# Query features of the last three batches taken token-major and turned by the DMA crossbar, in a kernel of linear attention and a squared-ReLU layer

## The chip, the cores and the metric

The kernel runs on one core of a Trainium2 chip. The metric is the time of one execution on the device, in microseconds (us). The kernel before took 355.43 us, the median of three runs (355.03 to 355.8).

## The reference

The program is attention with learned exponential features, and behind it a two-layer network without bias. Inputs are q, k and v of 8 batches, 8 heads, 576 positions and 64 values per head, a feature matrix `w_phi` of 64 x 128, and the network's weights of 512 x 2048 and 2048 x 512.

```python
def phi(x):
    proj = np.einsum('bhsd,df->bhsf', x, w_phi)
    proj = proj - np.max(np.abs(proj), axis=-1, keepdims=True)
    return np.concatenate([np.exp(proj), np.exp(-proj)], axis=-1)
q_p, k_p = (phi(q), phi(k))
kv = np.einsum('bhsf,bhsd->bhfd', k_p, v)
z = np.sum(k_p, axis=2)
num = np.einsum('bhsf,bhfd->bhsd', q_p, kv)
den = np.einsum('bhsf,bhf->bhs', q_p, z)[..., None] + 1e-06
attn = num / den                       # 8 x 8 x 576 x 64
x = attn.transpose(0, 2, 1, 3).reshape(4608, 512)
out = np.maximum(x @ w_in, 0.0) ** 2 @ w_out
```

So a token's query is projected on 128 features, and the exponentials of the projection and of its negative are the two halves of its features. The shift by the largest absolute value needs that maximum for each token and head.

## The kernel before, in words

A batch has 576 positions: 512 in four groups and 64 left over. The attention of a batch works in chunks c = 0 to 4. Chunks 0 to 3 hold 128 tokens by 8 heads, as 4 columns of 128 by 2 halves (a pair of heads lies on the upper and the lower 64 partitions); chunk 4 holds the 64 tokens that are left, two heads stacked on the partitions.

For batches 2 to 7, k and q are loaded by POOL's DMA queue (L253, L261, L273) into `xk` and `xq`, two buffers each (batch b uses buffer b % 2), and turned to `kT` and `qT` by one DMA transpose for each tensor, issued by SP (`transposed`, L338). Then:

- **Keys** (`kgroup_ops`): TensorE projects a group token-major (`project`, L354: 8 matmuls of 64 rows, two heads at a time on the two halves of the array), VectorE takes the maximum (L409), ScalarE writes the two exponentials `kp` and `kn` (L415). `em_ops` and `v_ops` scale v by the exponential of the maximum into `va`; `kv_ops` (L472, L477) sums over the tokens, into `kv`.
- **Query maxima** (`qmax_ops`): the same projection token-major (L354, called Pq here), VectorE's maximum (L514, Mq), and ScalarE's exponential of minus twice the maximum (`en`, L521, L527). The projection is then thrown away.
- **Query features** (`q_ops`): TensorE projects the same queries a second time, now with the features on the partitions (L549, called Fq: two matmuls of 64 rows by 512 columns, 256 in chunk 4), and ScalarE writes the exponentials `qp` and `qn` (L564), 3 slots of each, used in turn.
- **Output** (`out_ops`): `qp` times `kv` on TensorE (L579, NA: 8 matmuls), VectorE multiplies the sum by `en` (L591, SA), `qn` times `kv` is added (L579, NB), VectorE divides (L599, L603) into `xo`, and SP turns `xo` by a DMA transpose (L637, Xx) into `xT`, or for chunk 4 into `xS`.

Batches 0 and 1 are turned on TensorE (L328) instead.

The network (`ffn_in`, L719, F1: four matmuls of 128 x 512 for one piece; `ffn_out`, L784, F2: four more) runs over chunks of 512 tokens. Chunk c of 0 to 7 is made of batch c's first 512 positions and needs all four pieces of `xT` before its first F1; chunk 8 is made of the 64 positions left in each batch (`xS`). `relu_sq` (L694, L696, L703) is between F1 and F2. Results leave through `ot` (L195, L197; 3 buffers) and a store that SP issues (L803).

Each operation is first recorded by `add` as a step with a number, in the order of the program. Then the lists at the end of the file decide: `ORDER` is the one sequence in which all 1731 steps are emitted, so it fixes each engine's own order (engines run in order and meet only on semaphores); `BASES` is the PSUM bank of each accumulation; `STATES` picks VectorE, ScalarE or GpSimd where a step may go to either; `GATES` ties single POOL loads to an earlier step. Attention of batch b + 1 is spread between the F1 and F2 steps of chunks b and b - 1.

Of the kernel before, what the change touches and what calls it, by code (L numbers as in the profile page):

```python
# [7 lines left out]
F32 = mybir.dt.float32  # L8
# [3 lines left out]
ACT = mybir.ActivationFunctionType  # L12
# [12 lines left out]
def dve_cost(n):  # L25
    return n / 960 + 0.064, n / 960 + 0.150 + SEM
# [85 lines left out]
def kernel(  # L112
# [41 lines left out]
    def sb(name, shape, dt=BF16):  # L154
        return pool.tile([P, *shape], dt, name=name)

    def ring(name, n, shape, dt=BF16):
        return [sb(f"{name}{i}", shape, dt) for i in range(n)]
# [19 lines left out]
    qp, qn = ring("qp", NQP, [8 * P]), ring("qn", NQP, [8 * P])  # L178
# [4 lines left out]
    mkn = sb("mkn", [36], F32)  # L183
# [132 lines left out]
    def attention(b):  # L316
# [181 lines left out]

        def qmax_ops(c):
# [17 lines left out]
            add("DVE", dve_cost(2 * n * Fd), fn, r=[pj], w=[("mq", s2, c)], closes=pj, what="Mq")  # L517
# [13 lines left out]

        qfeat = {}
# [128 lines left out]
        else:  # L661
# [17 lines left out]
            kv_ops(3)  # L679
            for c in range(5):  # L680
                qmax_ops(c)
            for c in range(5):
                q_ops(c)
                out_ops(c)
# [320 lines left out]
```

## Time and profile before

| | before |
|---|---|
| time, median of 3 runs | 355.43 us |
| span of the profiled execution (first to last instruction) | 353.0 us |
| median run less that span | 2.4 us |
| instructions | 8396 |
| TensorE matmul, weight load | 340.7 us, 192.2 us busy |
| VectorE, ScalarE, GpSimd | 276.1 us, 226.8 us, 96.6 us busy |
| DMA queue filled by software (POOL's loads) | 18.36 MB |
| DMA queue filled by hardware (SP: transposes and stores) | 20.42 MB |

In the profile PE is TensorE's matmul, PEld its weight load, DVE VectorE, ACT ScalarE, POOL GpSimd, and SPq the queue of DMA issues of SyncE. L549 is line 549 of the kernel. A row of a timeline gives start, length, engine, line, operation, tiles written and read, and count; in brackets stands the idle time of the engine before it and what ended that. Neighbouring instructions of one kind are merged in a row. Ends of matmuls are modelled, so the distance between two starts says more than a duration.

### The profile page before, as it was taken

How to read it: one execution, taken by the hardware profiler on the slowest of the kernel's cores; microseconds unless marked ns; L12 is line 12 of the kernel's file. 1: busy time of each engine (PE TensorE's matmuls, PEld its weight loads, DVE VectorE, ACT ScalarE, POOL GpSimd, SP SyncE). 2: the span in 40 equal slices, each digit the busy share in tenths (PEclk: the TensorE clock that was granted, in tenths of full speed). 3: DMA queues.
4: the chain of work that ended last, by engine and by line, in shares of the span. 5: the costliest groups of instructions: out<-in, count | busy, mean ns of one | idle time of the engine just before them, and what ended most of it. 6: DMA issues, size and time to landing. Idle time of an engine off the chain costs nothing.

```text
span 353.0 us, 8396 instructions
## 1 busy us (share of the span) xinstructions
PE 340.7 (97%) x3367; PEld 192.2 (54%) x3400; DVE 276.1 (78%) x524; ACT 226.8 (64%) x428; POOL 96.6 (27%) x144
## 2 busy tenths in 40 slices
PE   8889999999999999999999999999999999999995
PEld 5679875544654554545445654455555544444452
DVE  4999998899979988989678888799988727736210
ACT  4999887499688875785678577869676211340301
POOL 8745350488429300297001820000000000000000
PEclk9999999999999999999999999999999999999999
DMA  9999999899989976899354995600211211010105
GB/s 102 177 200 202 196 107 155 134 142 175 182 169 150 155 141 155 160 111 158 79 129 84 120 187 111 146 20 21 53 40 53 47 51 48 30 59 2 59 3 176
DMA packets 96101, 39.59 MB, mean 112 GB/s; under 512 B 64576, under 2 KB 91584, under 8 KB 96064
## 3 DMA queue, kind: packets, MB, share of 16 engines
q0 software_dynamic: 45216, 18.36, 45.6%
q1 hardware_dynamic: 50528, 20.42, 26.5%
q8 instruction: 26, 0.43, 0.5%
q10 hardware_dynamic: 320, 0.30, 0.3%
q14 instruction: 11, 0.09, 0.1%
HBM read 36.77 MB, written 9.44 MB: 131 GB/s over the span
## 4 chain that ended last, share of the span: by engine, by line
PE 79%; DVE 8%; ACT 6%; DMA 3%; issue 2%; SPq 0%; POOL 0%; DVEq 0%; ACTq 0%; POOLq 0%
PE psum L784 30%; PE psum L719 28%; PE psum L579 5%; PE psum L354 4%; PE psum L472 3%; PE psum L730 3%; PE psum L549 2%; DVE va L442 2%; DMA xq<-in_q_dram 1%; DVE mq L514 1%; ACT kp L415 1%; ACT kn L415 1%; DMA out_dram<-ot 1%; DVE mk L388 1%; DVE h L703 1%
## 5 line engine op out<-in xcount | busy, mean ns | idle before, releaser
L784 PE MATMUL psum<-wout,h 128*128 128x512 bf16 x527 | 128.4, 379 | 3.2 <-issue 1.3
L719 PE MATMUL psum<-xT,win 128*128 128x512 bf16 x448 | 106.1, 379 | 0.1
L694 ACT ACTIVATE hr<-psum 128x512 bf16<-128x512 f32 x96 | 55.3, 596 | 46.3 <-PE psum L719 24.3
L784 PEld LDWEIGHTS <-h 128*128 128x128 bf16 x560 | 50.2, 98 | 55.2 <-issue 2.0
L719 PEld LDWEIGHTS <-win 128*128 128x128 bf16 x512 | 47.4, 97 | 53.7 <-issue 3.1
L703 DVE TENSOR_TENSOR h<-hr 128x512 bf16<-128x512 bf16 x143 | 55.9, 415 | 16.4 <-ACT hr L694 15.6
L564 ACT ACTIVATE qp<-psum 128x1024 bf16<-128x1024 f32 (+1 forms) x40 | 37.4, 940 | 21.9 <-PE psum L549 21.5
L514 DVE TENSOR_REDUCE mq<-psum 128x8 f32<-128x1024 f32 (+1 forms) x40 | 44.1, 1110 | 4.0 <-PE psum L354 3.2
L409 DVE TENSOR_REDUCE mk<-psum 128x8 f32<-128x1024 f32 (+1 forms) x35 | 38.1, 1110 | 3.1 <-PE psum L354 3.1
L415 ACT ACTIVATE kp<-psum 128x1024 bf16<-128x1024 f32 (+1 forms) x35 | 32.8, 937 | 11.6 <-DVE mk L409 8.9
L564 ACT ACTIVATE qn<-psum 128x1024 bf16<-128x1024 f32 (+1 forms) x40 | 37.4, 939 | 1.3 <-PE psum L579 1.0
L696 DVE TENSOR_SCALAR hr<-psum 128x512 bf16<-128x512 f32 x48 | 32.6, 686 | 6.5 <-PE psum L719 5.2
L253 POOL DMA_DIRECT2D xv<-in_v_dram x26 | 19.4, 763 | 51.3 <-DVE va L442 48.0
L415 ACT ACTIVATE kn<-psum 128x1024 bf16<-128x1024 f32 (+1 forms) x35 | 32.8, 936 | 0.0
L442 DVE TENSOR_TENSOR va<-xv,va 64x256 bf16<-64x256 bf16 (+2 forms) x68 | 30.4, 462 | 1.6 <-ACT va L434 0.8
L591 DVE TENSOR_TENSOR psum<-psum,en 128x520 f32<-128x520 f32 (+1 forms) x40 | 27.6, 699 | 3.9 <-PE psum L579 2.5
L603 DVE TENSOR_TENSOR xo<-psum,rden 128x512 bf16<-128x512 f32 (+1 forms) x40 | 27.3, 686 | 1.0 <-DVE rden L599 0.2
L197 ACT ACTIVATE ot<-psum 128x512 f32<-128x512 f32 x18 | 10.7, 595 | 27.1 <-PE psum L784 27.1
L195 DVE COPY ot<-psum 128x512 f32<-128x512 f32 x17 | 11.5, 684 | 15.2 <-PE psum L784 7.9
L253 POOL DMA_DIRECT2D xk<-in_k_dram x28 | 20.6, 743 | 8.4 <-ACT va L428 4.0
L472 PE MATMUL psum<-va,kp 128*128 128x65 bf16 x256 | 19.6, 193 | 0.8 <-DVE va L442 0.4
L472 PE MATMUL psum<-va,kn 128*128 128x65 bf16 x256 | 19.6, 193 | 0.0
(69 smaller groups left out, 403.4 us busy)
## 6 DMA issues: line engine op xcount, KB each, us to landing
out_dram<-ot SPq DMA_DIRECT2D x32, 256.0 KB, 2.7
xk<-in_k_dram POOLq DMA_DIRECT2D x26, 128.0 KB, 4.3
xq<-in_q_dram POOLq DMA_DIRECT2D x24, 128.0 KB, 5.5
xv<-in_v_dram POOLq DMA_DIRECT2D x24, 128.0 KB, 4.2
win<-in_moe_w_in_dram POOLq DMA_DIRECT2D x4, 512.0 KB, 11.3
wout<-in_moe_w_out_dram POOLq DMA_DIRECT2D x4, 512.0 KB, 11.7
xq<-in_q_dram POOLq DMA_DIRECT2D x4, 256.0 KB, 5.8
xv<-in_v_dram POOLq DMA_DIRECT2D x2, 512.0 KB, 9.3
```

What stands on the lines that cost most here:

```text
L253: pin(nc.gpsimd.dma_start(out=x[:, a * 512 : z * 512].rearrange("p (h x) -> p h x", x=4 * D), in_=src[b][2 * a : 2 * z, 0:512, :].rearrang ...
L409: pin(nc.vector.tensor_reduce(out=mk_view(g), in_=ps2(pj)[:, :, : n * Fd].rearrange("p e (i f) -> p e i f", f=Fd), axis=AX.X, op=ALU.max, ...
L415: pin(nc.scalar.activation(out=dst[slot][:, :, :n, :].rearrange("p e i f -> p e (i f)"), in_=ps2(pj)[:, :, : n * Fd], func=ACT.Exp, scale= ...
L442: pin(engine().tensor_tensor(out=t[:, :, :D].rearrange("p m (x c) -> p m x c", c=2), in0=x.rearrange("p (m x c) -> p m x c", m=n, c=2), in ...
L472: pin(nc.tensor.matmul(out=o[:, sg, hi, :], lhsT=(kp, kn)[sg][kgroup[pr]][:, j % 2, 2 * hi + j // 2, :], rhs=va[s2][sg][:, 8 * pr + 4 * hi ...
L514: pin(nc.vector.tensor_reduce(out=mqb[:, c, :, :n], in_=ps2(pj)[:, :, : n * Fd].rearrange("p e (i f) -> p e i f", f=Fd), axis=AX.X, op=ALU ...
L564: pin(nc.scalar.activation(out=o, in_=i_, func=ACT.Exp, scale=sgn))
L694: pin(nc.scalar.activation(out=hr[sl], in_=ps1(g), func=ACT.Relu))
L696: pin(nc.vector.tensor_scalar(out=hr[sl], in0=ps1(g), scalar1=0.0, scalar2=None, op0=ALU.max))
L703: pin(engine().tensor_tensor(out=dst, in0=i_, in1=i_, op=ALU.mult))
L719: pin(nc.tensor.matmul(out=o, lhsT=win[mc // 4][:, kc, mc % 4 * P : (mc % 4 + 1) * P], rhs=x, start=(kc == 0), stop=(kc == KC - 1)))
L784: pin(nc.tensor.matmul(out=ps1(g), lhsT=h2[c % 2][mc // 4][:, mc % 4, tt * P : (tt + 1) * P], rhs=wout[mc // 4][:, mc % 4, :], start=(mc = ...
```

## The change

For batches 5, 6 and 7 (`LATE = 5`) the second projection goes. After Mq, ScalarE takes both exponentials straight from the token-major projection in PSUM, whose banks so stay taken until the second one has read them. It writes them into the batch's own `xk` (chunks 0, 2, 4) or `xq` buffer (chunks 1, 3), whose contents have been turned into `kT` and `qT` by then. SP then issues a DMA transpose from there into the slot of `qp` and `qn`, which are now two halves of one tile `qf`: one transpose of 128 x 2048 for chunks 0 to 3, two of 128 x 512 for chunk 4. That step is called Xf. NA waits for it. In the same batches a chunk's maximum, features and output are recorded chunk by chunk.

So 15 Fq steps go and 15 Xf steps come; the number of steps stays 1731. The unused tile `mkn` goes. `ORDER`, `BASES` and `STATES` are the same for the first 780 steps and new behind them; step 780 of the sequence lies in the middle of batch 4's attention. Of `GATES`, the two entries of batch 7's loads 1365 and 1371 change their step (1027 to 1030, 1043 to 1201).

```diff
+    LATE = 5
+    qf = ring("qf", NQP, [2, 8 * P])
+    qp, qn = [t[:, 0, :] for t in qf], [t[:, 1, :] for t in qf]
-    qp, qn = ring("qp", NQP, [8 * P]), ring("qn", NQP, [8 * P])
...
+            turned = b >= LATE
+            add("DVE", dve_cost(2 * n * Fd), fn, r=[pj], w=[("mq", s2, c)] + [pj] * turned, closes=None if turned else pj, what="Mq")
+            if turned:
+                slot = qslot[0] % NQP
+                qslot[0] += 1
+                qfeat[c] = slot
+                src, qx = (("xk", xk), ("xq", xq))[c % 2]
+                qe = qx[s2][:, : 16 * P].rearrange("p (u x) -> p u x", u=2)
+                held = of(src, b, (0, 1, 2, 3, "s"))
+                for u, sgn in enumerate((1.0, -1.0)):
...
+                        pin(nc.scalar.activation(out=o, in_=i_, func=ACT.Exp, scale=sgn))
+                    add("ACT", act_cost(2 * n * Fd), fn, r=[pj], w=[pj] + held, closes=pj if u else None, what="Eq")
...
+                        for u in range(2):
+                            pin(nc.sync.dma_start_transpose(out=qf[slot][:, u, : 4 * P].rearrange("f (x p) -> f x p", p=P),
+                                                            in_=qe[:, u, : 4 * Fd]))
...
+                        pin(nc.sync.dma_start_transpose(out=qf[slot].rearrange("f u (x p) -> f (u x) p", p=P),
+                                                        in_=qx[s2][:, : 16 * P]))
+                add("SP", (2.5 if c < 4 else 2.0, 0), fn, r=held, w=[("qp", slot), ("qn", slot)],
+                    dma=(3.2 * n / 4, HW_IN, "x", "kq"), what="Xf")
...
-            for c in range(5):
-                qmax_ops(c)
             for c in range(5):
-                q_ops(c)
+                if b < LATE:
+                    q_ops(c)
+                else:
+                    qmax_ops(c)
                 out_ops(c)
```

More of the change, by code (lines that the diff above doesn't have):

```diff
@@ L182 @@
     xS = sb("xS", [4, KC, P])
-    mkn = sb("mkn", [36], F32)
     hr = ring("hr", 4, [TCH])
@@ L497, in q_ts @@
             return [(8 * (c // 2) + 4 * (c % 2) + i) if pe_in else 8 * (c % 2) + 2 * i + c // 2 for i in range(4)]
+        qfeat = {}
         def qmax_ops(c):
@@ L516, in fn @@
                     axis=AX.X, op=ALU.max, apply_absolute_value=True))
-            add("DVE", dve_cost(2 * n * Fd), fn, r=[pj], w=[("mq", s2, c)], closes=pj, what="Mq")
+            turned = b >= LATE
[8 more added lines that the diff above has]
+                for u, sgn in enumerate((1.0, -1.0)):
+                    def fn(u=u, sgn=sgn):
+                        i_, o = ps2(pj)[:, :, : n * Fd], qe[:, u, : 2 * n * Fd]
+                        if c == 4:
+                            o, i_ = o.rearrange("p (i e f) -> p e i f", e=2, f=Fd), i_.rearrange("p e (i f) -> p e i f", f=Fd)
+                        else:
+                            o = o.rearrange("p (e x) -> p e x", e=2)
+                        pin(nc.scalar.activation(out=o, in_=i_, func=ACT.Exp, scale=sgn))
+                    add("ACT", act_cost(2 * n * Fd), fn, r=[pj], w=[pj] + held, closes=pj if u else None, what="Eq")
+                def fn():
+                    if c == 4:
+                        for u in range(2):
+                            pin(nc.sync.dma_start_transpose(out=qf[slot][:, u, : 4 * P].rearrange("f (x p) -> f x p", p=P),
+                                                            in_=qe[:, u, : 4 * Fd]))
+                    else:
+                        pin(nc.sync.dma_start_transpose(out=qf[slot].rearrange("f u (x p) -> f (u x) p", p=P),
+                                                        in_=qx[s2][:, : 16 * P]))
+                add("SP", (2.5 if c < 4 else 2.0, 0), fn, r=held, w=[("qp", slot), ("qn", slot)],
+                    dma=(3.2 * n / 4, HW_IN, "x", "kq"), what="Xf")
             if c < 4:
@@ L530, in qmax_ops @@
                     add("ACT", act_cost(4), fn, r=[("mq", s2, 4)], w=[("en", s2, 4, hi)], what="en")
-        qfeat = {}
         def q_ops(c):
@@ L679, in attention @@
             kv_ops(3)
+            if b < LATE:
+                for c in range(5):
+                    qmax_ops(c)
             for c in range(5):
-                qmax_ops(c)
-            for c in range(5):
-                q_ops(c)
+                if b < LATE:
+                    q_ops(c)
+                else:
+                    qmax_ops(c)
                 out_ops(c)
@@ L948 @@
     '7762205543351613247724322302602306674447442731320126074760270660422244446264622606176160063720462403'
-    '6376440226246040224115440556605777123504024764140002202442402462567677750767766755006425602422242222'
-    '6400041712301603166777067742404660026444202224400017210165317677737366646061634664004006640006224525'
-    '2454225454357220664133466404400220620232550535444304162615557154625737570741465213753727542242756523'
-    '160'
+    '6376440226246040224115440556605777123504024764140002202442402462567677750767766755402201467400642646'
+    '4266227776716100460014544502020423226026604654504300515140113621064260665742202040442702345011443702'
+    '7542250627660666642226202014330305450141630654442067652643316674361775116140761614406327'
 )
@@ L955 @@
     '0000000000000000010100110100110100010010000010000010000000000000100000001000100010100111000000001000'
-    '0010000000001010000000100010000101010000100010010001001001111111000110010000001000110100100101000010'
-    '011000000101100101001001111100011100100101111010010100010000111111000100001'
+    '0010000000001010000000100010000101010011001000010000110000001100010010001110100010000001110111100110'
+    '010000001010111100010010110010011001011000000000111011110000100100010100011'
 )
```

166 rows, old and new, of tables (GATES, ORDER) are left out of this document.

## The prediction

> **What bounds the kernel now.** I read the page first: the busy times, the clock, the chain that ended last.
>
> ```profile
> span 353.0 us, 8396 instructions
> PE 340.7 (97%) x3367; PEld 192.2 (54%) x3400; DVE 276.1 (78%) x524; ACT 226.8 (64%) x428; POOL 96.6 (27%) x144
> PEclk9999999999999999999999999999999999999999
> PE 79%; DVE 8%; ACT 6%; DMA 3%; issue 2%; SPq 0%; POOL 0%; DVEq 0%; ACTq 0%; POOLq 0%
> ```
>
> TensorE is busy 97% of the span at full clock and holds 79% of the chain. Busy time of pipelined matmuls says too little, so I went to starts in the timeline, and to TensorE's waits from 130 us on, where the new order begins to act: the first transpose behind step 780, batch 4's q, is the second of the two that start at 127.61 us.
>
> ```profile
> 163.36 1.02 PE L719 MATMUL psum<-xT,win 128*128 128x512 bf16 x4
> 164.31 0.10 PEld L549 LDWEIGHTS <-wphi 64*128 64x128 bf16 x2 [0.42 <-issue]
> ...
> 343.38 2.59 PE psum L784 x12
> ```
> ```profile
> PE psum L784 <- issue: 1.0, 6, 0.2
> PE psum L784 <- DVE ot L195: 0.7, 1, 0.7
> PE psum L579 <- DVE psum L591: 0.2, 1, 0.2
> ```
> ```profile
> 127.61 5.64 SPq L338 DMA_TRANSPOSE qT<-xq  x2
> ...
> 236.96 0.53 SPq L803 DMA_DIRECT2D out_dram<-ot  x1
> ```
>
> Twelve matmuls of 512 columns follow each other in 2.59 us, 0.216 each; that is the pace of an array that never waits. From 130 us to the end TensorE waited for another engine twice, 0.9 us in all. So a microsecond of matmul taken out there is a microsecond of the end, unless a new wait takes its place; and a better order alone can win at most about 1 us.
>
> The Trainium skill ("Trainium Kernel Development and Optimization", Performance Expectations) calls matmul busy time a bad metric for closeness to the roofline "because matmuls are pipelined" and would look at the weight loads, 54% here. By that reading TensorE would have slack and the change would give nothing; the starts 0.216 us apart decide against it.
>
> **What goes.** The second projection of a chunk, and what it costs in starts:
>
> ```profile
> 158.58 0.28 PE L549 MATMUL psum<-qT,wphi 64*128 64x256 bf16 x2
> 158.80 0.39 PE L719 MATMUL psum<-xT,win 128*128 128x512 bf16 x1
> ...
> 247.55 0.39 PE L549 MATMUL psum<-qT,wphi 64*128 64x512 bf16 x2
> 247.78 0.39 PE L354 MATMUL psum<-wphi,qT 64*128 64x128 bf16 x8
> ...
> 248.00 0.39 PE L354 MATMUL psum<-wphi,kT 64*128 64x128 bf16 x8
> ...
> 248.32 1.90 PE L784 MATMUL psum<-wout,h 128*128 128x512 bf16 x8
> ```
>
> The two matmuls of 512 columns run side by side on the halves of the array: 0.23 us from their start to the next one (247.55 to 247.78). For chunk 4 it is 0.22 us, in which the way back to full-height matmuls lies. That way can be priced: eight L354 matmuls take 0.22 us when eight more follow and 0.32 when L784 follows, so leaving costs 0.10. Entering costs about as much: four L719 from 163.36 end at 164.22, L549 starts at 164.31, 0.09 later. So a stretch of half-height matmuls costs 0.19 us besides its work, and chunk 4's pair 0.12.
>
> - 12 pairs x 0.23 + 3 x 0.12 = **3.1 us** of TensorE.
> - Stretches: going through both ORDER lists behind step 780, I count 24 in the old one and 20 in the new. 4 x 0.19 = **0.8 us**.
>
> **What is moved or added.** ScalarE and VectorE do the same work: 30 exponentials of 1024 or 512 columns out of PSUM move from L564 to the new line.
>
> ```profile
> 247.98 1.02 ACT L564 ACTIVATE qp<-psum 128x1024 bf16<-128x1024 f32 x1 [1.39 <-PE psum L549]
> 248.27 1.23 DVE L514 TENSOR_REDUCE mq<-psum 128x8 f32<-128x1024 f32 x1 [0.52 <-PE psum L354]
> ```
>
> PSUM gets easier: the projection's two banks are held 2 x 1.02 us longer, but Fq's two banks, held as long, are not taken. So these cost nothing by themselves. Each chunk gains a DMA step, which the trace does not show in this size; its neighbours on both sides are:
>
> ```profile
> L338 SPq DMA_TRANSPOSE qT<-xq x6: 2671/2784/7034, 50.2 to 217.4; - x6
> DMA to landing us min/median/max: 4.6/5.4/11.0
> ```
> ```profile
> L637 SPq DMA_TRANSPOSE xT<-xo x28: 1188/1217/2485, 60.5 to 283.9; - x28
> DMA to landing us min/median/max: 2.3/2.8/6.5
> ```
> ```profile
> out_dram<-ot SPq DMA_DIRECT2D x20, 256.0 KB, 2.6
> ...
> xk<-in_k_dram POOLq DMA_DIRECT2D x8, 128.0 KB, 4.4
> ...
> xT<-xo SPq DMA_TRANSPOSE x19, 2.5
> ...
> xS<-xo SPq DMA_TRANSPOSE x5, 3.8
> qT<-xq SPq DMA_TRANSPOSE x4, 4.8
> kT<-xk SPq DMA_TRANSPOSE x3, 4.6
> ```
>
> xT is 4 blocks of 128 x 128, qT 18; Xf has 16. So SP is held 1.2 to 2.8 us by one, and it lands 2.5 to 4.8 us after its issue (the last fence, from 130 to 300 us; 11.0 at worst over the run). I take 2.5 and 4.6, nearer to 18 blocks. Chunk 4 takes two of 4 blocks: 2.4 on SP, 3.7 to land. Between 130 and 300 us SP issues 7 large and 24 small transposes and 20 stores of 0.53 us: 7 x 2.8 + 24 x 1.2 + 20 x 0.53 = 59 of 170 us. To these come 12 x 2.5 + 3 x 2.4 = 37. So SP is not full; the question is only whether something is late.
>
> Who waits: NA waits for Xf; behind a waiting Xf on SP stand stores of results, the transposes of `xo` and the next batch's q transpose, and behind those the first F1 of a chunk and VectorE's copies into `ot`. For this I added up TensorE's starts along the new ORDER (0.86 for an F1 or F2, 0.25 for NA or NB, from sixteen in 0.50 below, 0.23 for a projection) and compared with what must fit between:
>
> ```profile
> 246.79 0.21 DVE L599 RECIPROCAL rden<-psum 128x8 f32<-128x8 f32 x1 [0.18 <-PE psum L579]
> ...
> 247.07 0.68 DVE L603 TENSOR_TENSOR xo<-psum,rden 128x512 bf16<-128x512 f32 x1
> ...
> 250.06 0.66 PE L579 MATMUL psum<-kv,qp 128*128 128x65 bf16 x16
> ...
> 250.56 1.02 PE L784 MATMUL psum<-wout,h 128*128 128x512 bf16 x4
> ```
>
> - Projection to NA (batch 7, chunk 3, the shortest): TensorE has 10.4 us of other work. Needed: 0.23 + 1.23 + 2 x 1.02 + 4.6 + 0.4 for hand-overs (my estimate) = 8.5. Spare 1.9.
> - A slot of `qf` free to the NA that reads its next content (batch 6, chunk 0 to 3): 7.0 us of work, 0.2 + 4.6 needed. Spare 2.2 if nothing else holds SP.
> - Last NB to the chunk's first F1: in the old order 7.5 to 9.8 us of work, in the new 5.2 to 6.5. Needed: 0.2 + 0.21 + 0.68 + 2.5 + 0.4 = 4.0. Spare 1.2 in place of 3.5.
>
> So the new order fits when landings are at their medians, but with some ten places of 1 to 2 us spare where the old one had 3 or more. A single transfer can be 2 to 6 us beyond its median (11.0 against 4.8). I price waits at **+1.2 us** over today's: three places late by 0.4. Bounds: below nothing, since the old order's own 0.9 us of waits can go (-0.9), and +6 when one landing of 11 us meets a spare of 2 and others follow.
>
> POOL: batch 7's loads now wait until batch 5's Xf have been read out of `xk` and `xq`.
>
> ```profile
> 192.47 0.71 POOL L253 DMA_DIRECT2D xv<-in_v_dram  x1 [27.41 <-DVE va L442]
> ...
> 204.09 0.72 POOL L273 DMA_DIRECT2D xq<-in_q_dram  x1
> ```
>
> The whole batch goes out in 12 us. In the new order batch 5's last Pq lies 35 us of TensorE work ahead of batch 7's first key projection; 3 us to Xf, 3.7 to land, 9.4 for thirteen loads, 4.4 and 4.6 for load and transpose make 25. Covered by 10 us; nothing.
>
> **Sum.** 355.43 - 3.1 - 0.8 + 1.2 = **352.7 us**. Against the profiled execution: its span of 353.0 (the median is 2.4 longer) becomes 350.3.
>
> **Rivals.**
>
> - *The waits eat the gain.* For: every spare above shrank. Against: the medians fit. Waits of 2.4 to 4.4 us in all give 353.9 to 355.9. Chance 0.20 (0.08 of it still faster by over 0.2%, 0.12 within 0.2%; 0.2% is about what a measurement of this kernel can tell).
> - *Slower: SP's queue holds the features.* In the new order SP has batch 7's q transpose, then Xf of batch 6's chunk 3, then stores and all four xT transposes of batch 6. The first waits for batch 7's last q load, the 17th of its 18. I reckon some 4 us between that landing and the moment NA needs the feature. From 4 us late on, TensorE stands still microsecond for microsecond, in NA and then in chunk 6's first F1. Such a hold-up exists today:
>
> ```profile
> 175.61 0.69 DVE L195 COPY ot<-psum 128x512 f32<-128x512 f32 x1 [2.11 <-DMA out_dram<-ot]
> ```
>
>   The store behind transposes on SP came late, `ot` was not free, and TensorE lost the 0.7 us quoted at the top. Now SP's issues grow by two thirds. One landing 8 us late instead of 4 gives +4, with the ordinary +1.2: 356.7; a second such place 358 to 359. Chance 0.22.
> - *The clock falls.* A wait long enough to lower TensorE's clock would cost twice.
>
> ```profile
> PE psum L853 <- DVE warm L234: 1.1, 1, 1.1
> ```
>
>   That is TensorE's longest wait, at the start, and the clock row stays at 9, so the traces so far speak against it. If a late transfer of the former rival stops TensorE for 4 us and it then runs at half pace for as long (an assumption, no row shows it), 2 us of matmuls take 4: 356.7 + 2 = 358.7. Chance 0.04. The Trainium skill ("TensorE: Matmul & The Clock Gate", Part 1) puts the threshold at an idle window of about 3.4 us and the lower clock at half.
> - *VectorE becomes the bound.*
>
> ```profile
> 215.00:260.00 45.00, 44.30 (x438) 23.32 (x441) 40.29 (x69) 35.12 (x67) 0.00 (x0) 1.00 0.29 71
> ```
>
>   PE, PEld, DVE and ACT here are busy 44.3, 23.3, 40.3 and 35.1 of 45 us, in the stretch of batches 6 and 7. Taking 1.4 us from TensorE leaves VectorE at 92%; hand-overs could then keep half the gain: 354.2. Chance 0.04.
>
> **How the numbers follow.** Forecast, 351.5 to 353.9: 0.50. Adding the parts of the rivals: faster 0.50 + 0.08 + 0.04 = 0.62, same 0.12, slower 0.22 + 0.04 = 0.26. The range goes from 351.2 (the 0.9 us of old waits gone, too) to 357.4, which cuts off the second late place and the clock; up to 2 in 10 is left out.
>
> **What would show it.** L549 falls from 80 matmuls to 50; L354 keeps its count. A new ACT line has 30 exponentials of 1.0 and 0.6 us; SPq has 18 new transposes, the large ones some 2.5 us on SP and 4.6 to land. TensorE's waits behind 130 us: under 2.5 us if I am right; a wait of L579 for the features, or of L719 for xT, of more than 2 us shows the slower rival, and PEclk below 9 the clock. I am wrong about the gain if L354's half-height stretches got more, not fewer, and about the waits if the large transposes land after 6 us or more beside batch 7's loads.

## The result, and the profile after

The changed kernel takes **364.74 us** (median of 6 runs, 362.82 to 365.25) against 355.23 us for the kernel before on the same chip (6 runs, 354.76 to 356.91). The ratio is 1.0256, 95% interval 1.0233 to 1.0279. It is slower by 9.5 us, where 2.7 us less were forecast.

The page of the changed kernel, the rows that answer to those of before:

```profile
span 362.8 us, 8408 instructions
PE 342.1 (94%) x3334; PEld 193.5 (53%) x3370; DVE 273.2 (75%) x521; ACT 228.2 (63%) x431; POOL 96.8 (27%) x144
...
PEclk9999999999999999899999999969999999999999
...
PE 72%; DMA 9%; ACT 8%; DVE 6%; issue 3%; POOL 1%; DVEq 0%; ACTq 0%; POOLq 0%
```

The span has grown by 9.8 us. Read the shares against before: TensorE has gone from 97% to 94% of the span, DMA from 3% to 9% of the chain, and two slices of the clock row are below 9. So time went into waiting for transfers, and some into a slower clock. TensorE's waits from 130 us on say for which transfers; the columns are the total, the count and the longest:

```profile
PE psum L355 <- DMA kT<-xk: 4.9, 2, 3.7
PE psum L355 <- DMA qT<-xq: 2.7, 1, 2.7
PE psum L751 <- ACT ot L198: 1.3, 2, 0.7
PE psum L816 <- issue: 1.2, 6, 0.3
PE psum L751 <- ACT hr L726: 0.2, 1, 0.2
```

These are 9.1 us of waits for other engines, against 0.9 before; the `issue` row (1.2 us here, 1.0 before) names no other engine. Look at what is *not* there: no wait of L607 (the line of NA and NB) for the new feature transposes. TensorE waits for the old ones, `kT` and `qT`, which the change does not touch. They stand at two places.

**Place A, 139 to 154 us.** POOL's loads, SP's q and k transposes, and TensorE in the changed kernel:

```profile
125.51 0.63 POOL L262 DMA_DIRECT2D xv<-in_v_dram  x1
...
131.10 0.64 POOL L262 DMA_DIRECT2D xk<-in_k_dram  x1
```
```profile
128.07 5.28 SPq L339 DMA_TRANSPOSE qT<-xq  x1
135.00 6.11 SPq L339 DMA_TRANSPOSE qT<-xq  x1
```
```profile
144.09 0.62 PE L355 MATMUL psum<-wphi,qT 64*128 64x128 bf16 x16 [2.72 <-DMA qT<-xq]
...
152.41 0.29 PE L355 MATMUL psum<-wphi,kT 64*128 64x128 bf16 x4 [1.18 <-DMA kT<-xk]
...
153.89 2.32 PE L751 MATMUL psum<-xT,win 128*128 128x512 bf16 x10 [0.75 <-ACT ot L198]
```

From 125.51 to 131.10 POOL issues nine loads of batches 5 and 6. In the kernel before POOL issued nothing between 125.0 and 145.67 us:

```profile
145.67 0.70 POOL L253 DMA_DIRECT2D xv<-in_v_dram  x1 [20.63 <-DVE va L442]
```

There the two q transposes held SP for 2.8 us each. Now they hold it for 5.28 and 6.11 us, and TensorE stands at 141 us for batch 4's `qT`. The stores of `ot` queue behind these transposes on SP, and the chain that ended last runs through two of these stores (issued at 141.20 and 147.92 us) to the last wait of the place.

**Place B, 226 to 242 us.** Batch 7's last k loads and its k transpose:

```profile
220.45 0.62 POOL L262 DMA_DIRECT2D xv<-in_v_dram  x1 [7.60 <-ACT va L429]
221.05 1.41 POOL L254 DMA_DIRECT2D xk<-in_k_dram  x2
```
```profile
226.72 5.57 SPq L339 DMA_TRANSPOSE kT<-xk  x1
```
```profile
235.92 0.82 PE L355 MATMUL psum<-wphi,kT 64*128 64x128 bf16 x12 [3.71 <-DMA kT<-xk]
237.08 4.77 PE L816 MATMUL psum<-wout,h 128*128 128x512 bf16 x11 [0.34 <-issue]
```

A v load of batch 7 waits on POOL for batch 6's `va`, the two last k loads stand behind it, and the k transpose so comes at 226.72, with six more loads just ahead of it. The wait is not for data. The load is step 1371, and its entry in `GATES`, one of the two that the change moves, ties it to step 1201, the last of batch 6's small `va` exponentials. That exponential was held up in turn: ScalarE stood 1.71 us until the feature transpose issued at 210.14 us had read `xq`, and this one landed after 8.69 us, beside eight loads that POOL issued from 207.6 to 212.9. So a new transpose is on the chain here after all, though TensorE did not wait for it. Before, all of batch 7's loads were issued by 204.8 us, and this k transpose started earlier and held SP for half as long:

```profile
220.27 2.69 SPq L338 DMA_TRANSPOSE kT<-xk  x1
```

After the wait come 11 matmuls of 512 columns in 4.77 us, 0.43 each where 0.216 is full pace. The table by stretches shows why; the column behind the five engines is the granted clock:

```profile
145.00:150.00 5.00, 4.51 (x25) 1.88 (x26) 3.26 (x5) 4.46 (x10) 2.30 (x4) 0.66 1.06 164
...
235.00:240.00 5.00, 3.75 (x19) 1.76 (x21) 2.63 (x4) 2.58 (x6) 0.00 (x0) 0.50 1.06 239
```

The clock falls behind both places, to 0.66 and 0.50 as means of 5 us. And the landings from 130 to 310 us (last column, median us from issue to landing):

```profile
qf<-xk SPq DMA_TRANSPOSE x12, 5.0
...
qf<-xq SPq DMA_TRANSPOSE x6, 4.3
...
qT<-xq SPq DMA_TRANSPOSE x4, 7.5
kT<-xk SPq DMA_TRANSPOSE x3, 7.8
```

By their medians the new transposes land about as forecast (4.6); the old ones take 7.5 and 7.8 us where they took 4.8 and 4.6.

### The profile page after: what moved, and what is told of

Same layout as the page of the kernel before. It is cut to its first block, busy times and chain, and to the rows that moved or that the text cites. A ratio compares the mean times of both kernels' runs of the same rounds, so it can differ in the third digit from the quotient of the medians.

```text
span 362.8 us, 8408 instructions
## 1 busy us (share of the span) xinstructions
PE 342.1 (94%) x3334; PEld 193.5 (53%) x3370; DVE 273.2 (75%) x521; ACT 228.2 (63%) x431; POOL 96.8 (27%) x144
## 4 chain that ended last, share of the span: by engine, by line
PE 72%; DMA 9%; ACT 8%; DVE 6%; issue 3%; POOL 1%; DVEq 0%; ACTq 0%; POOLq 0%
PE psum L816 27%; PE psum L751 26%; PE psum L607 5%; PE psum L355 4%; PE psum L762 3%; PE psum L473 3%; DMA kT<-xk 3%; DMA qf<-xq 2%; DMA out_dram<-ot 2%; DVE va L443 2%; ACT qf L592 2%; PE psum L577 1%; DVE mk L410 1%; ACT kn L416 1%; ACT kp L416 1%
## 5 line engine op out<-in xcount | busy, mean ns | idle before, releaser
L816 PE MATMUL psum<-wout,h 128*128 128x512 bf16 x524 | 133.1, 386 | 3.1 <-issue 1.5
L751 PE MATMUL psum<-xT,win 128*128 128x512 bf16 x448 | 107.7, 379 | 1.6 <-ACT ot L198 1.3
L726 ACT ACTIVATE hr<-psum 128x512 bf16<-128x512 f32 x91 | 52.6, 596 | 56.0 <-PE psum L751 46.1
L816 PEld LDWEIGHTS <-h 128*128 128x128 bf16 x560 | 51.5, 99 | 57.2 <-issue 5.3
L592 ACT ACTIVATE qf<-psum 128x1024 bf16<-128x1024 f32 (+1 forms) x50 | 46.0, 939 | 8.2 <-PE psum L577 7.9
L728 DVE TENSOR_SCALAR hr<-psum 128x512 bf16<-128x512 f32 x53 | 35.7, 685 | 13.1 <-PE psum L751 11.8
L607 PEld LDWEIGHTS <-qf 128*128 128x128 bf16 x640 | 28.2, 97 | 13.3 <-issue 1.4
L607 PE MATMUL psum<-kv,qf 128*128 128x65 bf16 x640 | 30.9, 193 | 0.0
L198 ACT ACTIVATE ot<-psum 128x512 f32<-128x512 f32 x26 | 15.6, 599 | 21.1 <-PE psum L816 12.6
L262 POOL DMA_DIRECT2D xq<-in_q_dram x16 | 10.3, 647 | 36.7 <-DMA qT<-xq 12.8
```

What stands on the lines that cost most here:

```text
L592: pin(nc.scalar.activation(out=o, in_=i_, func=ACT.Exp, scale=sgn))
L607: pin(nc.tensor.matmul(out=o[:, u // 4, u % 4 * D1 : (u % 4 + 1) * D1], lhsT=(qp, qn)[sg][slot][:, u * m : u * m + P], rhs=kv_sb[s2][:, h ...
L726: pin(nc.scalar.activation(out=hr[sl], in_=ps1(g), func=ACT.Relu))
L728: pin(nc.vector.tensor_scalar(out=hr[sl], in0=ps1(g), scalar1=0.0, scalar2=None, op0=ALU.max))
L751: pin(nc.tensor.matmul(out=o, lhsT=win[mc // 4][:, kc, mc % 4 * P : (mc % 4 + 1) * P], rhs=x, start=(kc == 0), stop=(kc == KC - 1)))
L816: pin(nc.tensor.matmul(out=ps1(g), lhsT=h2[c % 2][mc // 4][:, mc % 4, tt * P : (tt + 1) * P], rhs=wout[mc // 4][:, mc % 4, :], start=(mc = ...
```

## The experiments

Three theories. **Crowding**: POOL's loads, which the new order puts beside the q and k transposes, slow these down, and that is the loss. **Feature transposes**: the 18 new transposes fill SP's queue or the DMA engines, and everything behind them is late. **Clock**: half of the loss is the slower TensorE after the waits. Ratios are against the kernel before on the same chip.

### The loads of place A held back

```diff
+_behind([977, 1161, 1163, 1159, 974, 978, 1160, 975, 1162], 982)   # takes steps out of ORDER and puts them behind one
-977: 630
+977: 982
```

> The nine loads of batches 5 and 6 that go out at 125 to 131 us in the changed kernel are held back until VectorE has taken batch 5's first key maximum (some 143 us). Theory 1, loads crowd the transposes of q and k: batch 4's q transpose holds SP about 3 us instead of 6.1 and lands in about 5 instead of 9 us, TensorE's waits at 141 to 154 us (2.7, 1.2 and two of 0.6 to 0.8) and the low clock at 145 to 150 us go, the wait at 232 us stays: 358 to 360 us. Theory 2, the new feature transposes fill SP and the DMA queue: the first of them is issued at 173 us, so nothing changes at 141 us by moving loads beyond their own delay: 363 to 366 us.

361.04 us (359.12 to 361.89, 4 runs), ratio 1.0159, 1.0126 to 1.0193; 3.7 us less than the changed kernel by medians, and 1 us above what crowding expected. The q transposes are back at 2.95 and 2.68 us on SP, and no wait is left at place A. Place B is as it was, and a new wait of 2.5 us for `ot` has come at 170 us.

### Batch 7's last k loads put ahead of the v load that waits

```diff
+_behind([1356, 1355, 1373], 1359)
```

> Batch 7's last two k loads go ahead of the gated v load that held POOL's queue for 7.6 us, and SP issues batch 7's k transpose before two stores. Theory 1: the k transpose runs while no load does, lands in about 5 us instead of 9.2, before its first projection; TensorE's wait of 3.7 us at 232 us and the half clock behind it (2.4 us) go: 358 to 360 us. Theory 2: feature transposes of batch 6 stand ahead of it on SP all the same, so it stays late: 363 to 366 us.

358.14 us (357.8 to 359.67, 4 runs), ratio 1.0094, 1.0070 to 1.0117. The wait at 232 us and the slow clock behind it are gone; place A keeps a wait of 3.1 us for `qT`. Place B alone is worth 6.6 us by medians. The time is inside what crowding expected, but the way there was another. The k transpose was to run while no load does and land after about 5 us. It starts at 219.47 instead of 226.72 us, POOL issues seven loads from 219.1 to 224.3, and it lands after 7.4 us where it took 9.15. So most of what place B wins is the earlier start.

### Both

> Both edits together. Theory 1: both waits and both stretches of low clock go, what is left is the 3.9 us taken out of TensorE less some small waits: 351.5 to 354 us, faster than the kernel before. Theory 2: still slower than before, 358 us or more, with waits of the output products for the features.

357.47 us (354.9 to 359.69, 10 runs), ratio 1.0068, 1.0036 to 1.0099: less than the first, not to be told from the second, and not the 351.5 to 354 that crowding promised. One long wait is left in the profile:

```profile
PE psum L816 <- ACT ot L198: 3.8, 1, 3.8
```
```profile
165.24 0.56 SPq L835 DMA_DIRECT2D out_dram<-ot  x1
166.18 1.19 SPq L665 DMA_TRANSPOSE xT<-xo  x1
167.47 6.16 SPq L544 DMA_TRANSPOSE qf<-xk  x1
```

ScalarE waits until 173.5 us for the store of `ot` issued at 165.24, which lands only 8.2 us later. It stands ahead of the feature transpose in SP's queue, so that queue did not delay it. Near it now stand this transpose, with 6.16 us on SP, and 21 loads, shifted to between 147.9 and 163.2 us. Which of the two is to blame decides between the first and the second theory; the next experiments were made for that.

### The loads alone, in the kernel before

No feature transpose exists here: the same nine loads, in the kernel before, where the changed one has them.

```diff
+_behind([977, 1161, 1163, 1159, 974, 978, 1160, 975, 1162], 979)   # in the kernel before
```

> The kernel before, with no feature transposes at all, and only the nine loads of batches 5 and 6 put on POOL where the changed kernel has them, behind batch 5's k transpose, so that they run from about 126 us instead of behind 145 us. Crowding by loads: the q transposes of batches 4 and 5 take 4.5 us or more on SP (2.8 before) and 6 us or more to land, TensorE waits for a q or k transpose at 139 to 153 us, and the time rises by 1 to 4 us to 356 to 359 us. The feature transposes are needed for the loss: the q transposes keep 2.8 to 3.3 us on SP, and the time stays at 354.6 to 355.7 us.

**362.84 us** (361.97 to 363.44, 5 runs), ratio 1.0212, 1.0198 to 1.0226. That is 7.6 us more, beyond the 1 to 4 expected. Its two q transposes, and the same two in the kernel with both orders mended (the tile's view; min, median and max):

```profile
L338 SPq DMA_TRANSPOSE qT<-xq x2: 5071/6324/7576, 127.8 to 133.0; - x2
...
DMA to landing us min/median/max: 10.4/11.6/12.9
```
```profile
L339 SPq DMA_TRANSPOSE qT<-xq x2: 2680/2771/2862, 128.1 to 132.5; - x2
...
DMA to landing us min/median/max: 4.8/5.3/5.8
```

With the loads beside them the transposes hold SP twice as long and land twice as late. TensorE then waits, longest for `ot`, whose store stands behind these transposes on SP (issued at 140.66 us for 133.36 before), and runs slowly afterwards:

```profile
145.48 0.58 PE L354 MATMUL psum<-wphi,qT 64*128 64x128 bf16 x7 [4.38 <-DVE ot L195]
146.00 5.01 PE L784 MATMUL psum<-wout,h 128*128 128x512 bf16 x12
```

Waits for other engines of 6.1 us against 0.9 before, and 12 matmuls in 5.01 us against 2.59: 5.2 + 2.4 = 7.6, all of the 7.6 us. Crowding by the loads needs no help from the change's own transposes.

### Feature transposes of a quarter size

In the mended kernel and in the changed one; both leave out three quarters of the late features.

```diff
-out=qf[slot].rearrange("f u (x p) -> f (u x) p", p=P),          in_=qx[s2][:, : 16 * P]
+out=qf[slot].rearrange("f u (x p) -> f (u x) p", p=P)[:, :4],   in_=qx[s2][:, : 4 * P]
```

(and a block of each half for chunk 4)

> The kernel with both orders mended (357.47 us), in which each feature transpose moves a quarter of its columns; it leaves out three quarters of the transposed q features of batches 5 to 7, whose places keep old values. The feature transposes fill SP's queue or the DMA engines: the 3.8 us wait at 170 us goes, and the time falls to 352 to 354.5 us. Crowding by loads alone: a wait of 2 us or more for a store stays at 170 us and the time is 356 to 358 us.

> The changed kernel (364.74 us) as it is, in which each feature transpose moves a quarter of its columns; it leaves out three quarters of the transposed q features of batches 5 to 7, whose places keep old values. The feature transposes are the cause: the time falls by 5 us or more, to 355 to 360 us. Crowding of the k and q transposes by the loads of the new order: the waits of 2.7 us at 144 us and 3.7 us at 232 us stay, and the time is 362 to 365 us.

The changed kernel with quarter transposes takes 364.23 us (361.57 to 365.29, 4 runs), ratio 1.0244, 1.0210 to 1.0278, not to be told from 1.0256. Its waits are at the same places, and no shorter:

```profile
PE psum L355 <- DMA kT<-xk: 6.0, 2, 4.3
PE psum L355 <- DMA qT<-xq: 3.1, 1, 3.1
```

The mended kernel with quarter transposes takes 356.81 us (353.6 to 358.11, 10 runs), ratio 1.0020, 0.9991 to 1.0050. In its profile the wait at 170 us is still 2.9 us, though the first feature transpose holds SP for only 1.27 us. So the size of the feature transposes explains nothing of the loss in the changed kernel, and of the rest some 1.7 us by the two ratios (1.0068 and 1.0020), whose intervals overlap. With that the size of the new transposes falls as the cause of the loss. Their number, their places in SP's queue and what waits for them were left as they are, so these runs say nothing of those.

### Matmuls that fill the two waits

Unused matmuls ahead of the two waiting projections (24 and 34 of 248 columns) keep TensorE busy, to hold the clock.

```diff
+            bank = op.opens[0].base if bank is None else bank
 FILL = {
+    831: (None, 24, 0), 1375: (None, 34, 0),
```

> The changed kernel with 24 and 34 unused matmuls of 248 columns ahead of the two projections that wait longest, into the PSUM bank that the projection itself opens; they write values that nobody reads. Theory 3, half of the loss is TensorE's clock falling after a long wait: the waits for the transposes stay, but the clock stays at 1.00 at 145 to 150 and 235 to 242 us, where eleven matmuls of 512 columns took 4.77 us instead of 2.38: 360.5 to 362 us. If the clock has no part, or if the waits themselves are all: 364 to 366 us.

365.03 us (363.74 to 367.65, 4 runs), ratio 1.0289, 1.0246 to 1.0332: no gain. The clock did stay at 1.00 in both stretches, but at place A the slow clock only moved behind the next wait:

```profile
153.74 0.29 PE L355 MATMUL psum<-wphi,kT 64*128 64x128 bf16 x4 [3.58 <-DMA kT<-xk]
...
155.14 5.22 PE L751 MATMUL psum<-xT,win 128*128 128x512 bf16 x16 [0.67 <-ACT ot L198]
```
```profile
239.06 2.76 PE L816 MATMUL psum<-wout,h 128*128 128x512 bf16 x12
```

At place B 12 matmuls take 2.76 us where 11 took 4.77, so the slow clock costs about 2.3 us there. At place A what the faster matmuls win, the next wait takes (3.58 us for 1.18): batch 5's `kT` is late in any case. Behind it 16 matmuls take 5.22 us, where they take 3.5 at full pace; the granted clock from 155 to 160 us is 0.66, as it was at 145 to 150 without the unused matmuls. And both places end later by the wall (153.74 for 152.41, 238.62 for 235.92 us), which takes the 2.3 of place B back. As a forecast of 360.5 to 362 us the third theory fails. But the edit took away only one of the two slow stretches, so what the clock costs apart from its wait stays open.

### Where to put the loads

Batch 6's six q loads, or three of its loads, out of the crowd at 148 to 163 us, in the mended kernel:

```diff
+_behind([1168, 1165, 1169, 1167, 1164, 1166], 1091)       # held to a relu;     1168: 211 -> 1091
+_behind([1168, 1165, 1169, 1167, 1164, 1166], 875)        # to 171 us;          1168: 211 -> 875
+_behind([1171, 1166, 1173], 875)                          # three of them;      1171: 916 -> 875
+_behind([973, 1168, 1165, 1169, 1167, 1164, 1166], 875)   # the second, with batch 5's v load 973
+_behind([973], 976)                                       # ahead of the six
```

> The kernel with both orders mended (357.47 us), and batch 6's six q loads moved on POOL from 154 to 161 us to behind a relu of expert 4 at 175 us, so that fewer loads stand beside the first feature transpose of batch 5 (6.16 us on SP at 167.47) and the store ahead of it, for which ScalarE and then TensorE waited 3.8 us. Crowding by loads: the transpose falls to 2.5 us or less on SP, the wait of F2 at 170 us to under 1 us, and the time to 352.5 to 354.5 us, below the kernel before; if the q loads come too late there, batch 6's q transpose at 186 us waits and 1 to 3 us come back. The feature transposes fill SP's queue by themselves: the transpose keeps 4 us or more, the wait stays over 2.5 us, and the time stays at 356.5 to 358.5 us.

361.8 us (361.22 to 363.21, 4 runs), ratio 1.0193. The place aimed at went as crowding says: with the six loads and one behind them gone the first feature transpose takes 2.02 us on SP instead of 6.16, and the wait of 3.8 us is gone. But POOL got to the loads only at 180.49 us, and the risk that was named came in, larger than the 1 to 3 us: TensorE waited for batch 6's `qT`.

```profile
194.70 0.61 PE L355 MATMUL psum<-wphi,qT 64*128 64x128 bf16 x8 [4.96 <-DMA qT<-xq]
```

> Both orders mended, and batch 6's six q loads behind the scaling of chunk 3 of batch 4 (VectorE at 170.4 us in the kernel that held them to 180.5 us), ten us earlier than there. Crowding by loads in time: the loads run at 171 to 176 us, batch 6's q transpose is issued at 185 to 187 us and its 5.0 us wait goes, the first feature transpose stays near 2 us on SP and the 3.8 us wait of F2 at 170 us is gone; 352.5 to 354.5 us, below the kernel before. If the loads only carry the crowding with them: the stores issued at 171 us or the second feature transpose at 176 us (1.9 us on SP there) take twice their time, TensorE waits 2 us or more for an output buffer or for features between 172 and 186 us, and the time is 355.5 to 358 us.

> Both orders mended, and only three of batch 6's loads (two of v, one of q) behind the same step at 170.4 us, so that 17 instead of 20 loads run from 148 to 160 us. If the crowd clears by degrees: the first feature transpose takes 2 to 4.5 us on SP (6.16), the wait of F2 at 170 us falls below 2 us, and the time is 353.5 to 355.5 us. If it clears only when the six are gone: the wait stays over 2.5 us, and the time at 356.5 to 358.5 us. If it is the features' own doing the count of loads changes nothing: 357 to 358 us.

362.76 us (361.85 to 363.64, 4 runs), ratio 1.0225, and 360.24 us (359.35 to 362.28, 4 runs), ratio 1.0146. Both lie above every time that was expected. In both the first feature transpose is at 2.0 us (2.04, 2.02) and the wait at 170 us gone. In the second POOL issued five of the 21 loads behind 171 us, the three and two that stand behind them, so five fewer were enough for that. Both tell little more, since the edit also pushed a v load of batch 5 behind the held ones, and VectorE waited 8.5 and 6.1 us for it. With that load put back:

> The kernel with batch 6's six q loads at 170.4 us (362.76 us), whose v load of batch 5 had been pushed behind them and held VectorE for 8.5 us, with that load put back ahead of them. Crowding by loads in time: the waits of 6.0 and 1.1 us at 178 to 187 us go with the half clock behind them, and the time is 352.5 to 355 us. If the six loads carry the crowd to 171 us: the second feature transpose at 176 us keeps 4 us or more on SP (7.40 there, 1.9 without loads), TensorE waits 2 us or more for the features behind it or for batch 6's q transpose, and the time is 356 to 360 us.

360.25 us (359.49 to 361.97, 6 runs), ratio 1.0156, 1.0127 to 1.0184. The six loads, and two behind them, carried the crowd to 171 us. SP and TensorE there:

```profile
176.08 7.45 SPq L544 DMA_TRANSPOSE qf<-xq  x1
```
```profile
183.62 1.87 PE L751 MATMUL psum<-xT,win 128*128 128x512 bf16 x4 [5.64 <-issue]
```

The row names no releaser. But the last transpose of `xT` ahead of this F1 was issued at 174.6 us and landed after 9.0 us, against a median of 2.5, and that is when the F1 starts. So here it is not q or k but another transpose that stands beside the loads.

### The loads earlier

One number of the mended kernel: POOL's held loads start at a maximum that is done at 143.1 us, behind batch 4's q transposes, instead of one at 147.6.

```diff
-977: 982
+977: 832
```

> Both orders mended (357.47 us), with one number changed: the first of POOL's held loads waits for a maximum on VectorE at 143.1 us, ahead of the one at 147.6, so that all 20 loads run some 4.7 us earlier, between the last q transpose of batch 4 and the first feature transpose. Crowding by loads in time: the loads are through before the feature transpose at 167 us, which falls from 6.16 us on SP to 3 us or less, the wait of F2 at 170 us falls below 1 us, and the time is 352.5 to 354.5 us, below the kernel before. If the crowd only moves: batch 5's k transpose or the two stores at 139 to 148 us land late, TensorE waits 2 us or more between 146 and 158 us, and the time is 356 to 361 us.

**352.98 us** (351.64 to 356.34, 12 runs), ratio 0.9950, 0.9922 to 0.9979: below both kernels, by 0.5% against the kernel before, and inside what crowding expected. Its page, its two longest kinds of waits from 130 us on, and SP at the place:

```profile
span 350.4 us, 8444 instructions
```
```profile
PE psum L816 <- ACT xq L536: 0.6, 1, 0.6
PE psum L577 <- ACT kn L416: 0.2, 1, 0.2
```
```profile
160.24 0.56 SPq L835 DMA_DIRECT2D out_dram<-ot  x1
165.75 1.19 SPq L665 DMA_TRANSPOSE xT<-xo  x1
167.05 2.01 SPq L544 DMA_TRANSPOSE qf<-xk  x1
```

The loads are issued by 159.1 us instead of 163.2, the feature transpose takes 2.01 us instead of 6.16, and no wait behind 130 us is longer than 0.6. All 18 feature transposes are there, at full size. Note what has not changed: from 130 to 310 us `qT` and `kT` still land after medians of 5.8 and 7.8 us, and TensorE waits for neither. A slow transpose costs only where its reader has no spare.

## Why the prediction was wrong

**The bound was right.** TensorE has no slack: in the kernel before with the nine loads moved, its waits and its clock make all of the 7.6 us.

**What goes was right in kind, and its size perhaps too large.** L549 (now L577) has 50 matmuls for 80, and from 130 us on the trace has 20 half-height stretches for 24. The kernel with the loads in place has a span of 350.4 us, and the working had 350.3; that the two meet is in part luck. The working counted +1.2 us for waits. By its trace that kernel waits 1.4 us for other engines from 130 us on, against 0.9 before, which is +0.5. So what went out of TensorE is worth about 2.6 + 0.5 = 3.1 us of the 3.9, by this estimate.

**What is moved or added: right in the medians.** The large feature transposes of the changed kernel (ns on SP: min, median, max):

```profile
L544 SPq DMA_TRANSPOSE qf<-xk x6: 1844/2474/4377, 173.6 to 273.8; - x6
L544 SPq DMA_TRANSPOSE qf<-xq x6: 1317/1920/3591, 182.2 to 282.0; - x6
```

The medians of 2.5 and 1.9 us, and 4.3 to 5.0 to land, stand against 2.5 and 4.6. TensorE never waited for the features in the changed kernel, and quarter transposes change nothing. But the sign that the working named for being wrong about the waits, a large transpose that lands after 6 us or more beside batch 7's loads, did come in: 8.69 us at 210.14. Its reader that waited was not NA but ScalarE, whose next exponential goes into the same `xq`; the working's list of who waits lacks it.

**The step that failed is the waits, "+1.2 us" with a bound of +6.** They came to 8.2 us more than before by the waits of TensorE for other engines (9.1 less 0.9), and the slower clock adds about 4 us (5 us at 0.66 make 1.7, the 11 matmuls at place B 2.3). With -3.9 that makes +8.3 of the span's +9.8, with -3.1 it makes +9.1; the rest I have not placed. The three spares that the step worked out are those of the features and of `xT`, and they held: `xT` still lands after a median of 2.5 us, and TensorE waited for neither. What the step lacks is a spare for `qT` and `kT`, the transposes that were there already; but for batch 7's `kT`, in the POOL step, waits for them were put at nothing, as if they would land after 4.8 and 4.6 us in any order. How long these transposes took depended on what stood beside them. The new order moved POOL's loads there, the medians went to 7.5 and 7.8 us, and at two places TensorE had no spare for that; at place B the transpose was issued late besides. I had taken 11.0 us, the worst landing in the kernel before, for an odd transfer, and not asked what stood beside it. The working shows it under the row of `qT`, but it is a k transpose, issued at 111.06 us in a run of loads that POOL issues without a pause from 103.5 to 115.3: the kernel before had shown the crowding already.

**The second failed step is POOL: "Covered by 10 us; nothing".** It asked only whether batch 7's loads come in time for their own consumer. It did not follow the nine loads of batches 5 and 6, which the new ORDER puts ahead of POOL's wait at 125 us, nor ask what any load does to a transfer beside it. Nor did it see that batch 7's last k loads stand behind a v load that the changed entry of `GATES` ties to batch 6's `va`. So the spare of 10 us at place B was not there either.

**The rivals.** "SP's queue holds the features" had the sign, but neither place nor mechanism: a stoppage at NA was expected, by batch 7's q transpose, and the stoppages were at projections of keys and queries. "The clock falls" was given 0.04 and happened, twice; its condition, a late transfer, was what I had priced too low. The assumption "half pace for as long" roughly fits place B: 3.7 us of waiting, then some 4.8 us at half pace. A slip in the range changes nothing here: with the old waits gone the terms give 355.43 - 3.9 - 0.9 = 350.6, not 351.2.

**What stays open.** That loads beside a transpose double its time is shown for place A, by the kernel before with nine loads moved. At place B the late start and the loads were not taken apart. Whether loads and transposes meet in the DMA engines, in the memory or in the queues is not shown: no experiment separated these. The mended kernels spread over 4 to 5 us from run to run (354.9 to 359.69, and 351.64 to 356.34 with the loads earlier), the kernel before over 0.7 to 3.2; I take it that some places still have little spare, but did not test it.

## What to carry to other kernels

Before adding DMA work to a kernel whose TensorE has no slack, lay all issuers of DMA on one time axis, those whose instructions the change only reorders too, and look for transposes beside bursts of loads; a duration read in the old order holds only for the old neighbours. Then work out a spare for every transfer that the new order moves or crowds, the old ones as well as the new. When a new order loses, see for which transfer TensorE waits: here it was one that the change did not touch. And put the suspect alone into the old kernel: the nine loads showed in one run what the profile of the changed kernel could not separate.

## What the runs showed of the hardware

- A DMA transpose of `qT` held SP for 2.7 to 2.9 us and landed after 4.8 to 5.8 us with no load issued beside it, and for 5.1 to 7.6 us with a landing after 10.4 to 12.9 us beside nine loads of POOL's queue. The transposes of `xT` went from a median of 2.5 to as much as 9.0 us. The cost falls on the queue that issues as well, and so on the stores behind: one of them was issued 7.3 us later (140.66 for 133.36 us).
- The clock does not follow from the length of a wait alone. One-microsecond stretches behind the wait of 2.72 us at place A, behind that of 3.77 us in the kernel with both orders mended, and behind that of 2.89 us at the same place with quarter transposes:

```profile
146.00:147.00 1.00, 1.00 (x4) 0.31 (x3) 1.00 (x2) 1.00 (x2) 1.00 (x2) 0.50 1.34 192
```
```profile
175.00:176.00 1.00, 1.00 (x9) 0.51 (x8) 0.12 (x1) 1.00 (x3) 0.00 (x0) 1.00 0.74 163
```
```profile
174.00:175.00 1.00, 1.00 (x4) 0.35 (x3) 0.00 (x0) 1.00 (x2) 0.00 (x0) 0.50 0.93 336
```

  The two shorter ones were followed by half clock, the longest one was not. The Trainium skill ("TensorE: Matmul & The Clock Gate", Part 1) speaks of an idle window of about 3.4 us; these three waits do not sort by their length against it.
